# Two tiles in turn for the key differences of shared maxima, the second at the place of a residual block that waits in memory

## The chip, the cores and the metric

The kernel runs on one core of a Trainium2 chip. The metric is the device time of one execution in microseconds (us), the median of three runs. The engines of the core have one instruction queue each: TensorE (PE for its matmuls, PEld for its weight loads), VectorE (DVE), ScalarE (ACT), GpSimd (POOL) and SyncE (SP), which issues all DMAs here. They run side by side and wait for each other through semaphores.

## The reference, cut to what matters

Four layers work on one sequence of S = 2048 rows of D = 576 numbers, all in float32, with H = 32 heads of Dh = 18. Layers 0 and 2 (A) have their own keys and values for each head, layers 1 and 3 (B) share one key and one value head among all 32 query heads.

```
x = x + A(layernorm(x));  x = x + B(layernorm(x))
x = x + A(layernorm(x));  x = x + B(layernorm(x))

A: q, k, v = (x @ wqkv), 32 heads of 18 each
B: q = x @ wq (32 heads), k = x @ wk, v = x @ wv (one head of 18)
scores = (q @ k.T) * 18 ** -0.5
p = softmax(scores, over the keys)
result = (p @ v, heads side by side) @ wo
```

The softmax subtracts each row's maximum, so a maximum over 2048 keys is wanted for each of the 32 x 2048 query rows before the exponentials of that row can be computed.

## The kernel before, in words

**Stages.** The residual x stays in SBUF for the whole kernel, as 16 blocks of 128 rows x 576 (the tile xo, block c is xo[:, c, :]). A layer has a projection stage (layernorm, q and k written to memory, v kept in SBUF), an attention stage, and an output projection that adds its result to xo block by block, block 15 last; this runs together with the next layer's beginning. Between the layernorm statistics of a layer and its output projection, no instruction of the kernel before reads or writes xo.

**Two passes over the scores.** Attention goes over 16 pairs of heads and, in each, over four stretches u of 512 queries: 64 stretches a layer. Each stretch needs 32 score matmuls for its maxima (items m: 128 queries x 512 keys, tile psm in PSUM, max_mm) and 32 for its exponentials (items e: 128 keys x 512 queries, tile pse, exp_mm). The maxima are made LEAD = 14 steps of four items ahead of the exponentials. An e goes through ACT (L826), which writes the exponential into a tile pt, one of a ring of 14; PE multiplies the pt with v into the accumulator oacc (L864). Of an m, DVE takes the maximum of each row (L606).

**Shared maxima.** For some pairs of key blocks the kernel uses max(s0, s1) = s0 + relu(s1 - s0). The matmul of the difference uses differences of keys, prepared on GpSimd (L590, in A layers for the pair of heads after). ACT writes the positive part into the tile relu in SBUF (L599), and a later m, the partner, adds it to its own scores and takes the maximum in one DVE instruction (L604, tensor_tensor_reduce, with a short read of the accumulator behind it). ACT so takes a share of what two DVE reductions would do. Only one tile relu is there: 128 x 512, in the ring "xh". ACT may write it only when the partner before has been consumed on DVE. The partner of a difference is the first item m of the same head that stands more than three items behind it.

**The order** on the engines is written out by hand in the table UNIT, whose round of ten rows makes 32 items m and 32 items e. In an entry such as r12, the letter is the kind (m, e, or r for the m whose matmul is a difference), the first digit is the head of the pair, the second is the rank of the PSUM bank to take, counted from the one used longest ago (`lru`, seven banks). The number behind a row is the count of columns of the product with v that follow the row on PE.

```
        ("e00 e10 m00 r12 m10 e01", 384),
        ("m00 e10 e01 m10 m11 r00", 448),
        ("e00 m10 e00 m01 e10 m01 e10", 416),
        ("e10 m00 m10 m10 e00 e10 e00", 416),
        ("m00 e10 e02 e10 m01 r10 m00", 352),
```

These are rows 5 to 9. A round holds three differences: r12 in row 5, whose partner is the m11 of row 6; r00 in row 6, whose partner is the first m00 of row 8; r10 in row 9. The two heads use different halves of the array's rows, so an item of head 0 and one of head 1 run side by side.

**Differences in the first stretches.** Differences are used from the third stretch of the first pair of heads on, so 62 of 64 stretches in each layer hold three of them: 62 x 3 x 4 = 744 in the kernel.

**Slots of pt.** `slot` chooses which tile of the ring the next exponential goes to. It keeps, in `wrote`, the tick at which each tile was last written by ACT, and in `seen` the last tick that ACT is known to have finished; a difference tile has an entry of its own there.

**The SP queue.** Stores and loads are issued in the program's order. The dictionary `todo` gives steps to them: `run_todo` issues all that is due at the present step, and a transfer that has to wait for another engine holds those behind it. At the start of an attention stage (step LEAD) the queue gets the loads of key differences (diff_in, L637), the constant rows of the next operands (L501, L504) and the next heads' rows (L510); at its end stand the parts of the last stretches (L888 to L910) and the first loads of the output projection (out_rows, L308 and L309).

Of the kernel before, what the change touches and what calls it, by code (L numbers as in the profile page):

```python
# [8 lines left out]
F32 = mybir.dt.float32  # L9
# [7 lines left out]
S, D, H = 2048, 576, 32  # L17
DH = D // H
P = 128
# [27 lines left out]
LEAD = 14  # L47
# [10 lines left out]

OUT_AHEAD = 2
TAIL = 2  # L60

# [18 lines left out]
def tile_kernel(ctx: ExitStack, tc: tile.TileContext, A_x, A_wqkv, A_wo, B_x, B_wq, B_wk, B_wv, B_wo, out):  # L82
    nc = tc.nc
# [6 lines left out]
    dram = ctx.enter_context(tc.tile_pool(name="dram", bufs=1, space=DRAM))  # L90
# [19 lines left out]
    xo = cst.tile([P, NCH, D], F32, name="xo")  # L110
# [25 lines left out]
    m_d = [dram.tile([4, 2, 4, P], F32, name=f"m_d{i}") for i in range(4)]  # L136
    o_d = dram.tile([D, S], F32, name="o_d")
    r_d = dram.tile([H, S], F32, name="r_d")

    rb = cst.tile([P, 512], F32, name="rb")  # L140

# [10 lines left out]
    def bank(i, name):  # L152
        lru.remove(i)
        lru.append(i)
        return psum.tile([P, 512], F32, tag=f"b{i}", bufs=1, name=name)
# [225 lines left out]
    def run_tail(n):  # L381

        for _ in range(n):
            if tail:
                for f, args in tail.pop(0):
                    f(*args)

    def out_proj(last):

        for c in range(NCH):  # L390
# [5 lines left out]
            if c >= OUT_AHEAD:  # L396
                run_tail(TAIL)
            if last and c == NCH - 1:
# [12 lines left out]
    for layer in range(4):  # L411
# [125 lines left out]
        def ops(p):  # L537
            return big[:, q_slot(p)], big[:, k_slot(p)]
# [11 lines left out]
        for a in range(2):  # L550
            n = -4 * LEAD % 32
# [10 lines left out]
        def max_place(a, i):  # L562

            p, u = divmod(i // 16, 4)
            if i < len(m_first):
                return (0, *m_first[i])
            n = i % 16
            return (p, u, *m_order[a][n]) if i >= 32 else (p, u, n // 2 % 4, n // 8 % 2 * 2 + n % 2)


        ns = STEPS * 4 * NPAIR
        m_heads = ([0, 1] * (2 * LEAD) + [a for _, a in UNIT_M] * (4 * NPAIR))[:4 * ns]

        def max_mm(bank=mtile):

            i = m_done[0]
            a = m_heads[i]
            p, u, qc, kb = max_place(a, m_next[a])
            q, k = ops(p)
            if (p, u) not in mxs:  # L580
                mxs[p, u] = pool.tile([P, 32], F32, name="mx") if (p, u) < (0, 2) else mx2[u % 2]
            mx, ps = mxs[p, u], bank("psm")
            by_act = reader[lru[-1]]
            reader[lru[-1]] = False
            b, r = 64 * a, 16 * a + 4 * qc + kb
            c0 = u * 512 + qc * P
            if (p, u) >= (0, 2) and (a, qc, kb) in m_diff:
                assert kd_pair[p % 2 if is_a and p else 2] == (p if is_a else 0)
                k = kd(p)[b:b + 3 * DH]
                nc.tensor.matmul(ps.rearrange("p (h t) -> p h t", h=2) if p == 0 or not is_a else ps,  # L590
                                 q[b:b + 3 * DH, c0:c0 + P], k,
                                 start=True, stop=True)
                t = relus[p, u, a, qc] = relu[:, :512]
                reader[lru[-1]] = True
                if not by_act:
                    seen[0] = max(seen[0], wrote.get("relu", -1))
                wrote["relu"] = ticks[0]
                ticks[0] += 1
                nc.scalar.activation(t, ps, AF.Relu)  # L599
            else:  # L600
                nc.tensor.matmul(ps, q[b:b + KM, c0:c0 + P], k[b:b + KM, kb * 512:(kb + 1) * 512], start=True, stop=True)  # L601
                if kb == 0 and (p, u, a, qc) in relus:
                    t = relus.pop((p, u, a, qc))
                    nc.vector.tensor_tensor_reduce(t, ps, t, 1.0, LOWEST, OP.add, OP.max, mx[:, r:r + 1])  # L604
                else:
                    nc.vector.reduce_max(mx[:, r:r + 1], ps, axis=AX.X)  # L606
            m_next[a] += 1
            m_done[0] += 1
            while m_full and i >= m_full[0][1] + 2:
                max_final(*m_full.pop()[0])  # L610
            m_count[p, u] = m_count.get((p, u), 0) + 1
            if m_count[p, u] == 32:
                assert m_next[0] == m_next[1]
                m_full.append(((p, u), i))

        relus, diffs, kd_pair = {}, {}, {}
        ring, free, wrote, seen, ticks = [], [], {}, [-1], [0]

        def kd(p):
            if p == 0 or not is_a:  # L620
                return big[:, 1::4, 7 * 256:]
            i = p % 2
            return xx_flat[:, 512 * i:512 * i + 512]
# [43 lines left out]
        def max_pairs():  # L667

            if is_a:
                run_todo(m_done[0] // 4)  # L670
            elif m_done[0] == 44:
                max_store(0, 0)
            elif m_done[0] == 48:
                max_rows(0, 0)
            for i in range(4):
                max_mm(etile if i == 3 else mtile)
            while m_full:
                max_final(*m_full.pop()[0])
# [116 lines left out]
        def max_final(p, u):  # L795
            neg = pool.tile([P, 8], F32, name="neg")
            nc.vector.tensor_reduce(neg, mxs.pop((p, u)).rearrange("p (b k) -> p b k", k=4), axis=AX.X, op=OP.max,  # L797
                                    negate=True)
            hl = nms[p, u] = hls[(4 * p + u) % 2]
            copy(nc.gpsimd, hl[:, 0:8], neg)  # L800
            nc.gpsimd.tensor_tensor(hl[:, 8:16], neg, hl.bitcast(F32)[:, 0:8], op=OP.subtract)
# [109 lines left out]


        relu, raw = (pool.tile([P, 640], F32, tag="xh", bufs=2, name=n) for n in ("relu", "raw"))
        todo = {}

        def at(b, f, *args):
            todo.setdefault(b, []).append((f, args))

        for p in range(NPAIR):
            for u in range(4):  # L920
                b = STEPS * (4 * p + u) + STEPS - 1
                if is_a or p or u:
                    at(b + NM_AT, max_store, p, u)
                    at(b + ROW_AT, max_rows, p, u)
                for d, f in ((SUM_AT, o_sum), (L_AT, l_part), (INV_AT, l_inv), (R_AT, l_out), (RB_AT, l_rows),
                             (MUL_AT, o_mul), (O_AT, o_out)):
                    at(b + LEAD + d, f, p, u)
            if p + 1 < NPAIR and is_a:
                for d, f in ((0, diff_in), (3, diff_split), (5, diff_out), (10 if p else 8, diff_rows)):
                    at(max(LEAD, 32 * p - 8) + d, f, p + 1)  # L930
            if is_a and p in (0, 1):
                at(LEAD + 20 + 32 * p, load_rows, q_slot(p + 1), 2 * (p + 1) * DH, DH, 1536, S)
            if p + 1 < NPAIR:
                for i in range(4 if is_a else 2):
                    at(LEAD + 32 * (p - 1) + 1 + 8 * i if p else LEAD + 1 + 4 * i, load_part, p + 1, i)
# [37 lines left out]
        while m_done[0] < 4 * ns:  # L973
            rows, cols = UNIT[phase % len(UNIT)]
            run_todo(LEAD + sum(e_next) / 4)
            for kind, a, rank in rows:
                if kind == "e":
                    exp_next(a, rank)
                elif m_done[0] < 4 * ns:
                    max_mm(oldest(rank))  # L980
            skip = min(cols, PV_LAG - lagged)
            lagged += skip
            pv_cols(cols - skip)
            phase += 1
# [47 lines left out]
```

## Time and profile before

| | us |
|---|---|
| median of three runs | 5727.78 |
| lowest and highest | 5721.95, 5728.45 |
| the profiled execution | 5725.34 |
| span of the profiled execution, first to last instruction | 5723.6 |

| engine | busy, us | share of the span |
|---|---|---|
| PE | 5606.4 | 98% |
| PEld | 3067.1 | 54% |
| DVE | 5026.7 | 88% |
| ACT | 4831.2 | 84% |
| POOL | 1842.7 | 32% |

The granted clock of TensorE was 0.999 on average. The first layer's attention lasts from about 220 to 1430 us, the second's from about 1595 us on.

How to read the rows: a group row names the line, the engine, the operation, its output and input tiles with their sizes and the count; behind it stand the busy time and the mean duration in ns, and, after the bar, how long the engine stood idle just before these instructions and what ended most of that. A row of the timeline gives the start in us from the span's start, the duration in us of all that it merges (the count is at the end, as x3), the engine and the line; in brackets stands the idle time of the engine ahead of it and the instruction whose end released it. A row of waits reads "engine, line <- who was waited for: us in total, times, longest". A window row gives, for each engine, busy time and count of instructions, then the granted clock, the DMA share and GB/s. Matmuls are pipelined and their ends are modelled.

### The profile page before, as it was taken

The numbers are of one execution on the slowest core, as the hardware profiler recorded it, in microseconds if no ns is written. First come the engines' busy times: TensorE is split into PE (matmuls) and PEld (weight loads), VectorE is DVE, ScalarE is ACT, GpSimd is POOL, SyncE is SP. The second block draws the span as 40 slices with busy tenths as digits, with TensorE's granted clock in tenths as the row PEclk, the third lists the DMA queues.
The fourth block names the chain that finished last, engine by engine and source line by source line (L and its number), as shares of the span: only waits on it lengthen the run. The fifth ranks groups of instructions, "written<-read, shape, count | busy, mean of one in ns | idle before, by whom it ended". The sixth has DMA issues, their size and how long they took to land.

```text
span 5723.6 us, 143368 instructions
## 1 busy us (share of the span) xinstructions
PE 5606.4 (98%) x55774; PEld 3067.1 (54%) x55774; DVE 5026.7 (88%) x9489; ACT 4831.2 (84%) x9624; POOL 1842.7 (32%) x2396
## 2 busy tenths in 40 slices
PE   9999999999999999999999999999999999999999
PEld 8644444444844444444686444444448444444446
DVE  4799999998699999999737999999977999999995
ACT  2599999999389999999626999999992999999996
POOL 3243333334233333323412433333342332323232
PEclk9999999999999999999999999999999999999999
DMA  6321111111421000000253211111114100000002
GB/s 204 120 59 41 42 46 44 43 44 27 130 62 26 23 24 20 21 23 24 60 172 102 55 46 41 44 44 46 38 38 132 51 24 23 24 24 20 23 15 79
DMA packets 276207, 303.69 MB, mean 53 GB/s; under 512 B 136270, under 2 KB 194214, under 8 KB 266238
## 3 DMA queue, kind: packets, MB, share of 16 engines
q1 hardware_dynamic: 275526, 294.53, 18.0%
q8 instruction: 438, 7.18, 0.5%
q14 instruction: 243, 1.99, 0.1%
HBM read 168.50 MB, written 121.95 MB: 51 GB/s over the span
## 4 chain that ended last, share of the span: by engine, by line
PE 85%; DVE 8%; ACT 3%; issue 2%; POOL 1%; DMA 0%; SPq 0%; ACTq 0%; POOLq 0%; DVEq 0%
PE oacc L864 33%; PE psm L601 21%; PE pse L822 19%; PE psn L259 6%; DVE mx L606 5%; PE psq L433 5%; ACT relu L599 3%; DVE relu L604 3%; PE psm L590 1%; ACT pt L826 0%; POOL ev L445 0%; PE ps L251 0%; DMA big<-qk_d 0%; POOL wsm L205 0%; PE oacc L252 0%
## 5 line engine op out<-in xcount | busy, mean ns | idle before, releaser
L826 ACT ACTIVATE pt<-pse 128x512 f32<-128x512 f32 x8192 | 4233.6, 620 | 104.8 <-PE pse L822 86.0
L606 DVE TENSOR_REDUCE mx<-psm 128x1 f32<-128x512 f32 x6704 | 4183.3, 684 | 81.6 <-PE pse L822 49.0
L601 PE MATMUL psm<-big 62*128 62x512 f32 x7448 | 2461.4, 430 | 91.5 <-ACT relu L599 88.8
L822 PE MATMUL pse<-big 64*128 64x512 f32 x8192 | 2537.5, 442 | 1.7 <-ACT evr L444 1.6
L864 PE MATMUL oacc<-pt,vbuf 128*19 128x416 f32 (+9 forms) x26544 | 1733.0, 368 | 4.6 <-DVE oc L176 4.0
L822 PEld LDWEIGHTS pse<-big 64*128 64x128 f32 x8192 | 1214.0, 184 | 796.8 <-DVE mx L606 370.6
L601 PEld LDWEIGHTS psm<-big 62*128 62x128 f32 x7448 | 1178.7, 185 | 687.2 <-ACT pt L826 251.9
L864 PEld LDWEIGHTS oacc<-pt,vbuf 128*19 128x19 f32 x26544 | 546.4, 97 | 792.4 <-issue 551.9
L176 POOL TENSOR_SCALAR hl<-neg 128x8 fp32r<-128x8 f32 x256 | 50.6, 197 | 2693.1 <-DVE neg L797 2693.1
L604 DVE CUSTOM_DVE_ANT_0 relu<-psm,relu 128x512 f32<-128x512 f32 x744 | 509.4, 685 | 175.7 <-ACT pt L826 173.6
L599 ACT ACTIVATE relu<-psm 128x512 f32<-128x512 f32 x744 | 452.1, 608 | 140.8 <-DVE mx L604 135.2
L864 PE MATMUL oacc<-pt,vy 128*19 128x384 f32 (+3 forms) x8176 | 570.1, 383 | 0.0
L892 POOL TENSOR_TENSOR rl<-lt,mone 128x8 f32<-128x8 f32 x256 | 422.3, 1650 | 297.6 <-DMA lt<-os 291.6
L176 POOL TENSOR_SCALAR os<-oc 32x512 f32<-32x512 f32 x512 | 313.2, 612 | 114.2 <-DVE oc L176 63.6
L441 ACT ACTIVATE ev<-psq 128x512 fp32r<-128x512 f32 (+1 forms) x112 | 66.9, 598 | 326.9 <-PE psq L433 222.8
L883 POOL TENSOR_TENSOR os<-os,oc 96x512 f32<-96x512 f32 x256 | 328.0, 1281 | 21.4
L905 POOL TENSOR_TENSOR os<-os,rb 96x512 f32<-96x512 f32 x256 | 328.7, 1284 | 18.9 <-DMA rb<-r_d 18.9
L259 PE MATMUL psn<-wsm,xx 128*128 128x288 f32 x2240 | 307.9, 296 | 1.3 <-issue 1.3
L259 PEld LDWEIGHTS psn<-wsm,xx 128*128 128x128 f32 x2240 | 298.7, 188 | 14.3 <-issue 12.3
L864 PEld LDWEIGHTS oacc<-pt,vy 128*19 128x19 f32 x8176 | 177.9, 98 | 229.4 <-issue 196.6
L447 DVE TENSOR_TENSOR ev<-psq,ev 128x512 fp32r<-128x512 f32 (+1 forms) x84 | 58.0, 691 | 213.9 <-ACT ev L441 202.6
L433 PE MATMUL psq<-yx,big 128*128 128x512 f32 (+2 forms) x826 | 197.1, 391 | 4.2 <-ACT yx L243 2.2
(93 smaller groups left out, 2391.5 us busy)
## 6 DMA issues: line engine op xcount, KB each, us to landing
big<-qk_d SPq DMA_DIRECT2D x172, 432.0 KB
qk_d<-ev SPq DMA_DIRECT2D x96, 512.0 KB
qk_d<-ev SPq DMA_DIRECT2D x120, 256.0 KB
rb<-r_d SPq DMA_DIRECT2D x512, 36.0 KB
o_d<-os SPq DMA_DIRECT2D x512, 36.0 KB
o<-o_d SPq DMA_DIRECT2D x64, 256.0 KB
xx<-qk_d SPq DMA_DIRECT2D x120, 72.0 KB
big<-m_d SPq DMA_DIRECT2D x512, 4.0 KB
```

The source lines that it names most:

```text
L176: eng.tensor_scalar(dst, src, 1.0, 0.0, op0=OP.mult, op1=OP.add)
L259: nc.tensor.matmul(ps, lhs[:, xc, :], wsm[:, wc, h * 288:(h + 1) * 288], start=i == 0, stop=i == len(TERMS) - 1)
L433: nc.tensor.matmul(ps[:n].rearrange("p (u t) -> p u t", u=2)[:, us], w[:, wc, :n], xts[T][:, us, xc, :], start=(xc, wc) == TERMS[0], stop= ...
L599: nc.scalar.activation(t, ps, AF.Relu)
L601: nc.tensor.matmul(ps, q[b:b + KM, c0:c0 + P], k[b:b + KM, kb * 512:(kb + 1) * 512], start=True, stop=True)
L604: nc.vector.tensor_tensor_reduce(t, ps, t, 1.0, LOWEST, OP.add, OP.max, mx[:, r:r + 1])
L606: nc.vector.reduce_max(mx[:, r:r + 1], ps, axis=AX.X)
L822: nc.tensor.matmul(e, k[r:r + KE, kc * P:(kc + 1) * P], q[r:r + KE, u * 512:(u + 1) * 512], start=True, stop=True)
L826: nc.scalar.activation(pt, e, AF.Exp, scale=SCALE)
L864: nc.tensor.matmul(oacc[j:j + DH + 1, cs], v_of(kc)[:, 2 * p + a if is_a else 0, :], pts[p, u, i][:, cs], start=kc < 2 and c0 == 0, stop=k ...
L892: nc.gpsimd.tensor_tensor(rl, lts.pop((p, u)), mone, op=OP.pow)
L905: nc.gpsimd.tensor_tensor(t[:96], t[:96], rb[:96], op=OP.mult)
```

## The change: what it does

The one tile relu becomes a list of two that are used in turn. The second is the first 512 columns of xo[:, 15, :], the last residual block. So that the block is free during attention, it is stored to a new tensor x_d in memory at step LEAD of each layer, ahead of what else is due at that step, and fetched at step LEAD + ns - 8 (ns = 512), when the last difference has been used. The first difference of each layer takes the place in xo. The tick bookkeeping for the ring of pt now has an entry for each of the two tiles. The matmuls, activations and reductions, and their order, are as before.

```
+AWAY = (15,)
...
+    x_d = dram.tile([len(AWAY), P, D], F32, name="x_d")
...
-                t = relus[p, u, a, qc] = relu[:, :512]
+                j = turn_r[0] = (turn_r[0] + 1) % len(relu)
+                assert all(n != j for n, _ in relus.values())
+                t = relu[j][:, :512]
+                relus[p, u, a, qc] = j, t
                 reader[lru[-1]] = True
                 if not by_act:
-                    seen[0] = max(seen[0], wrote.get("relu", -1))
-                wrote["relu"] = ticks[0]
+                    seen[0] = max(seen[0], wrote.get(-1 - j, -1))
+                wrote[-1 - j] = ticks[0]
                 ticks[0] += 1
                 nc.scalar.activation(t, ps, AF.Relu)
...
-                    t = relus.pop((p, u, a, qc))
+                    _, t = relus.pop((p, u, a, qc))
                     nc.vector.tensor_tensor_reduce(t, ps, t, 1.0, LOWEST, OP.add, OP.max, mx[:, r:r + 1])
...
-        relus, diffs, kd_pair = {}, {}, {}
+        relus, diffs, kd_pair, turn_r = {}, {}, {}, [0]
...
         relu, raw = (pool.tile([P, 640], F32, tag="xh", bufs=2, name=n) for n in ("relu", "raw"))
+        relu = [relu] + [xo[:, c, :] for c in AWAY]
...
+        def x_away():
+            for i, c in enumerate(AWAY):
+                nc.sync.dma_start(x_d[i], xo[:, c, :])
+
+        def x_back():
+            for i, c in enumerate(AWAY):
+                nc.sync.dma_start(xo[:, c, :], x_d[i])
+
+        at(LEAD, x_away)
+        at(LEAD + ns - 8, x_back)
```

## The prediction

> **What bounds the kernel now.** I read the page first: the busy times, the chain of waits, and the groups of the two operations that the edit touches.
>
> ```profile
> span 5723.6 us, 143368 instructions
> PE 5606.4 (98%) x55774; PEld 3067.1 (54%) x55774; DVE 5026.7 (88%) x9489; ACT 4831.2 (84%) x9624; POOL 1842.7 (32%) x2396
> PE 85%; DVE 8%; ACT 3%; issue 2%; POOL 1%; DMA 0%; SPq 0%; ACTq 0%; POOLq 0%; DVEq 0%
> PE oacc L864 33%; PE psm L601 21%; PE pse L822 19%; PE psn L259 6%; DVE mx L606 5%; PE psq L433 5%; ACT relu L599 3%; DVE relu L604 3%; PE psm L590 1%; ACT pt L826 0%; POOL ev L445 0%; PE ps L251 0%; DMA big<-qk_d 0%; POOL wsm L205 0%; PE o
> ...
> L604 DVE CUSTOM_DVE_ANT_0 relu<-psm,relu 128x512 f32<-128x512 f32 x744 | 509.4, 685 | 175.7 <-ACT pt L826 173.6
> L599 ACT ACTIVATE relu<-psm 128x512 f32<-128x512 f32 x744 | 452.1, 608 | 140.8 <-DVE mx L604 135.2
> ```
>
> TensorE (PE) is busy 98%, VectorE (DVE) 88%, ScalarE (ACT) 84%. The chain lies on PE for 85%, but a share leaves it: L606 and L604 on DVE, then L599 on ACT (5%, 3%, 3%). L599 is the ACT activation that writes the positive part of a difference block; L604 is the DVE instruction that reads it. Each runs 744 times, three in each of 248 rounds of the UNIT table.
>
> The window table over 1000 us of attention in an A layer and in a B layer shows an even state.
>
> ```profile
> 300.00:1300.00 1000.00, 981.08 (x10466) 486.71 (x10465) 950.26 (x1778) 948.03 (x1881) 360.02 (x457) 1.00 0.17 45
> 4600.00:5600.00 1000.00, 981.07 (x10469) 486.59 (x10466) 950.73 (x1781) 948.36 (x1882) 305.12 (x370) 1.00 0.09 21
> ```
>
> PE 981, DVE 950 and ACT 948 us of 1000, with the clock granted at 1.00. No engine is full, and none has more than 52 us per 1000 to spare. So I asked the table of waits who waits for whom.
>
> ```profile
> DVE relu L604 <- ACT pt L826: 173.6, 246, 0.7
> ACT relu L599 <- DVE mx L604: 135.2, 241, 0.6
> PE psm L601 <- ACT relu L599: 88.8, 244, 0.7
> ```
>
> ACT stands still ahead of L599 for 135.2 us in 241 waits, 0.56 us each, until L604 is done; PE then stands still for 88.8 us until L599 is done. About one such pair falls in each round. Two neighbouring rounds show where. First ACT, from the timeline:
>
> ```profile
> 2001.36 0.60 ACT L599 ACTIVATE relu<-psm 128x512 f32<-128x512 f32 x1
> 2001.84 1.60 ACT L826 ACTIVATE pt<-pse 128x512 f32<-128x512 f32 x3
> 2004.00 0.60 ACT L599 ACTIVATE relu<-psm 128x512 f32<-128x512 f32 x1 [0.56 <-DVE mx L604]
> 2004.49 5.58 ACT L826 ACTIVATE pt<-pse 128x512 f32<-128x512 f32 x11
> 2009.95 0.62 ACT L599 ACTIVATE relu<-psm 128x512 f32<-128x512 f32 x1
> ...
> 2023.12 0.60 ACT L599 ACTIVATE relu<-psm 128x512 f32<-128x512 f32 x1 [0.56 <-DVE mx L604]
> ```
>
> The round lasts 2023.12 - 2004.00 = 19.12 us. Of its three L599, those at 2001.36 and 2009.95 (r12 and r10 of the table) show no wait; the one at 2004.00 (r00) waits 0.56. DVE in the same stretch:
>
> ```profile
> 2003.22 0.68 DVE L604 CUSTOM_DVE_ANT_0 relu<-psm,relu 128x512 f32<-128x512 f32 x1
> ...
> 2003.90 1.98 DVE L606 TENSOR_REDUCE mx<-psm 128x1 f32<-128x512 f32 x3
> 2006.59 0.69 DVE L604 CUSTOM_DVE_ANT_0 relu<-psm,relu 128x512 f32<-128x512 f32 x1 [0.71 <-ACT pt L826]
> ...
> 2012.36 6.13 DVE L606 TENSOR_REDUCE mx<-psm 128x1 f32<-128x512 f32 x10 [0.19 <-PE pse L822]
> ```
>
> The L604 at 2003.22 consumes r12's tile and ends, with its 0.08 us read of the accumulator, at 2003.90; r00 begins 0.10 us later. The weights of r00's own matmul were loaded at 2002.02 (first row of the next fence), so only the tile held it. Later DVE waits 0.71 us, until 2006.59. Then the weight loads of PE (PEld), which show when PE reaches each burst of score matmuls:
>
> ```profile
> 2002.02 0.18 PEld L590 LDWEIGHTS psm<-big 54*128 54x128 f32 x1
> ...
> 2003.33 0.18 PEld L822 LDWEIGHTS pse<-big 64*128 64x128 f32 x1
> ...
> 2003.67 0.18 PEld L601 LDWEIGHTS psm<-big 62*128 62x128 f32 x1
> 2004.65 0.18 PEld L601 LDWEIGHTS psm<-big 62*128 62x128 f32 x1 [0.80 <-ACT relu L599]
> ...
> 2005.08 0.14 PEld L864 LDWEIGHTS oacc<-pt,vbuf 128*19 128x19 f32 x8 [0.25 <-issue]
> 2005.91 0.18 PEld L822 LDWEIGHTS pse<-big 64*128 64x128 f32 x1 [0.69 <-ACT pt L826]
> ...
> 2006.48 0.31 PEld L822 LDWEIGHTS pse<-big 64*128 64x128 f32 x2
> 2007.04 0.20 PEld L864 LDWEIGHTS oacc<-pt,vbuf 128*19 128x19 f32 x16 [0.25 <-issue]
> ```
>
> Table row 7 holds seven score matmuls and takes 2005.08 - 2003.33 = 1.75 us; row 8 holds seven as well, four for one half of the array and three for the other like row 7, and takes 2007.04 - 2005.91 = 1.13. The extra 0.62 us sits ahead of the load at 2004.65, which waits for L599: it takes over the PSUM bank of r00. The chain in each round is thus L604, L599, row 7, and everything behind it.
>
> **The change part by part.** *Second tile.* L599 takes two tiles in turn, so r00 no longer waits for the L604 at 2003.22 but for the one that read the other tile, about half a round earlier. Nothing is added to or taken from the instructions of PE, ACT and DVE. What comes free per round is read on each engine:
>
> - ACT: r00 could start when the three activations from 2001.84 have issued. That is at least 0.56 us earlier; up to 0.12 more, since activations overlap when nothing holds them (2001.36 to 2001.84 is 0.48 for a duration of 0.60).
> - PE: row 7 can shrink by 0.62, to the 1.13 of row 8. r00 would start between 2003.32 and 2003.44 and end by 2004.04; PE wants its bank at 2004.65 - 0.62 = 2004.03, so L599 is late there by 0.06 at most, with the hop to PE.
> - DVE: the work behind 2006.59 can come 0.71 earlier; then its gap is gone.
> - What is late next: in the bank order that the table gives, the sixth matmul of row 8 takes the bank of the sixth of row 7, the last of the three L606 from 2003.90, which end at 2005.88. That matmul's load is one of the pair at 2006.48. Moved by 0.62 it would come at 2005.86, before that bank is free; with the 0.05 us that L599's end at 2004.60 takes to reach the load at 2004.65, it can come at 2005.93. So the round shortens by 0.55.
>
> The value I take is 0.55 us in each of 248 rounds: 136 us. Bounds: 0.62 x 248 = 154 us if that bank costs nothing, and PE's own idle time, 88.8 us, if the burst has less slack than its loads show. Behind row 8 each engine keeps its present distance to the others, since all follow PE's shift; so I look for no new wait there.
>
> For the same wait the matmul's own row books 0.36 us of idle PE, where the loads show 0.62:
>
> ```profile
> 2004.65 0.50 PE L601 MATMUL psm<-big 62*128 62x512 f32 x1 [0.36 <-ACT relu L599]
> ```
>
> The Trainium skill ("Perfetto Trace Analysis", Identifying the Most-Contended Engine) says that the busy share of matmuls is a poor measure of how near TensorE is to its limit, because they are pipelined. By that rule the 88.8 us is no ceiling; against it, with PE's busy row taken at its word, the sum would be 88.8. The trace agrees with the rule so far as the two figures of this one wait differ.
>
> *Where the second tile lies, and its trips.* Residual block 15 is stored once a layer (x_away) and fetched once (x_back), 128 x 576 x 4 bytes = 288 KB each, on SP's queue. No engine instruction touches the block meanwhile. x_away goes in at the start of attention, ahead of the loads of L637:
>
> ```profile
> 219.71 0.33 SPq L469 DMA_DIRECT2D qk_d<-ev  x1
> 220.12 3.45 SPq L637 DMA_DIRECT2D xx<-qk_d  x4
> 225.76 0.61 ACT L599 ACTIVATE relu<-psm 128x512 f32<-128x512 f32 x1
> 1424.03 0.41 SPq L308 DMA_DIRECT2D o<-o_d  x1
> 1426.59 0.43 DVE L176 TENSOR_SCALAR xx<-o 128x512 fp32r<-128x512 f32 x1 [2.68 <-DMA o<-o_d]
> ```
>
> The first L599 of the layer, at 225.76, gets the new tile and so waits for x_away's landing. L309's and L308's 256 KB loads show the time of such a transfer: issued at 1424.03, used at 1426.59, 2.6 us. From 220.1 that gives 223 us, 2.7 us before it is wanted. I take nothing; the bound is twice the transfer, which still gives 225.3, and one more such transfer ahead of it, 3 us in each of four layers: 12 us. Behind x_away stand on SP the loads of L637 and the others of the next head pair, which shift by one issue, 0.3 to 0.8 us; the difference rows of pair 1 are wanted some 30 steps on, so nothing of it is seen. x_back comes at the end, when the difference tiles are no longer used; ahead of the o loads it can cost one issue and one transfer, some 0.4 + 2.6 us a layer, 12 us again. SP has room there: in the first layer it stands from 1416.58 to 1420.94.
>
> ```profile
> 1416.06 0.52 SPq L811 DMA_DIRECT2D big<-m_d  x2
> 1420.94 0.61 SPq L895 DMA_DIRECT2D r_d<-rl  x1
> ```
>
> So I take nothing. The block is wanted only by the last chunk of the output projection.
>
> *Slots.* The choice of the ring slot for exp tiles reads the tick of the tile's last L599, which is now older, so more activations may carry a wait of their own.
>
> ```profile
> L826 ACTq EVENT_SEMAPHORE  x876: 17/17/1129, 217.3 to 5657.5; - x176
> ```
>
> Such a wait takes 17 ns; one more a round is 4 us. I take nothing, with 4 us as the other bound, and as much to the good side if a slot choice comes out better.
>
> Sum, on the profiled execution's own time: it took 5725.3 us (span 5723.6 and 1.7 around it), and 5725.3 - 136 = 5589. It lay 2.5 us under the median of the three runs, 5727.8, so the forecast is 5591, or 2.4% less.
>
> **The rivals.** *Only PE's recorded idle time comes back.* If the matmuls behind the wait run at their limit in a way that the loads hide, 88.8 us is all: 5728 - 89 = 5639. For it: PE is busy 981 of 1000, and 0.36 x 248 = 89. Against it: rows 7 and 8 issue the same number of matmuls, and the 1.13 is seen in row 8 in the same round.
>
> *Row 8's bank costs nothing and overlap on ACT is won back too:* 0.62 a round, 5574.
>
> *The wait stays, or another takes its place in full.* The tile would be tracked together with the whole residual array, or r00 would be held by DVE's order through its bank: 5728. For it: DVE is busy 950 of 1000 and r00's release always coincides with L604. Against it: DVE has 0.71 + 0.19 us of gaps in the round, more than the 0.56, and the only users of the array during attention are L599, L604 and the two transfers.
>
> *Slower, by the clock.* The TensorE clock is granted by a regulator, and one stretch shows it low:
>
> ```profile
> 3072.00:3074.00 2.00, 2.00 (x14) 0.83 (x6) 0.77 (x2) 0.40 (x2) 0.00 (x0) 0.50 0.32 96
> ```
>
> At 0.50 for two us, with PE shown as busy throughout, ACT and DVE nearly stop. If a denser PE made such stretches common in attention, a round of 19.12 - 0.55 = 18.57 us at full clock would stretch; it is back at 19.12 at a mean clock of 18.57 / 19.12 = 0.971, and slower from there on: at 0.95 it is 19.55, 0.43 x 248 = 106 us over, 5834. Against it: in both windows above PE is already at 98% with 1.00 granted.
>
> **How the numbers follow.** Chances: the forecast with its own range of 5574 to 5610, 0.60; overlap won back, 5574 or a little below, 0.10; only the recorded idle time, near 5639, 0.15; wait stays, 0.07; slower, 0.04; the remaining 0.04 for losses at the layers' ends that leave between 5645 and 5716. Against no change I take a bound of 0.2%, 11 us, about what a measurement of this kernel can tell. Faster holds the first three and the last: 0.89. Same takes 0.06 of the case in which the wait stays, and slower its last 0.01 with the clock's 0.04: 0.05. The range runs from 5566 (154 and the 4 us of slots to the good, and the spread of the runs) to 5645 (the recorded idle time with some us of the layers' ends).
>
> **What would show it.** In the table of waits, ACT relu L599 <- DVE mx L604 should fall from 135.2 us to near nothing, PE psm <- ACT relu from 88.8 likewise. The round should be near 18.57 us, row 7 near 1.13 to 1.2 us, DVE's 0.71 us gap near 0.1, and row 8 should show up to 0.1 more. DVE and ACT should come to some 978 and 976 of 1000 (950 and 948 x 19.12 / 18.57). The first L599 of a layer should show no wait for a transfer. I am wrong if the round stays near 19.1 with another name in ACT's wait, if row 7 shrinks and another row grows by as much, or if the granted clock falls below 1.00 in attention.

## The result and the profile after

The changed kernel takes 5558.8 us (median of four runs, 5556.9 to 5563.9), the kernel before 5725.6 in the same comparison: a ratio of 0.971, with a 95% interval of 0.9694 to 0.9727. The profiled execution has a span of 5555.7 us, 167.8 less than before. The forecast was 5591 and the range began at 5566; the gain is larger than both allow. Of the kernels below, one (early_two) had one run of 19033.8 us among its six, far from the other five (5557.6 to 5560.6), and it is read by these five. First the page of the changed kernel, with the busy times and the chain of waits:

```profile
span 5555.7 us, 143125 instructions
PE 5524.8 (99%) x55774; PEld 3101.2 (56%) x55774; DVE 5001.2 (90%) x9489; ACT 4814.6 (87%) x9624; POOL 1844.3 (33%) x2396
PE 95%; issue 1%; POOL 1%; ACT 1%; DMA 1%; DVE 0%; SPq 0%; POOLq 0%; ACTq 0%; DVEq 0%
PE oacc L871 38%; PE pse L829 23%; PE psm L608 21%; PE psn L263 6%; PE psq L437 5%; PE psm L594 2%; ACT pt L833 0%; POOL ev L449 0%; PE ps L255 0%; DVE mx L613 0%; POOL wsm L209 0%; POOL big L209 0%; DMA big<-qk_d 0%; DMA qk_d<-ev 0%; POOL 
```

The chain has come back to PE: 95%, where it was 85%, and the DVE and ACT lines that made up the detour (5%, 3%, 3%) are gone. The change moved the lines: L599 is now L606, L604 is L611, L606 is L613, L601 is L608, L822 is L829, L826 is L833, L864 is L871. The window table over 1000 us of an A layer and of a B layer:

```profile
300.00:1300.00 1000.00, 997.68 (x10824) 510.72 (x10823) 978.18 (x1841) 978.38 (x1949) 374.99 (x479) 1.00 0.17 46
4450.00:5450.00 1000.00, 999.85 (x10860) 512.98 (x10858) 980.92 (x1847) 980.85 (x1955) 315.37 (x383) 1.00 0.09 22
```

DVE and ACT were forecast at 978 and 976 of 1000 and stand at 978 to 981; PE, at 981 before, is at 998 to 1000, all with the clock at 1.00. What ACT waited for ahead of the activation that writes a difference tile is told by the view of that line:

```profile
L606 ACT ACTIVATE xo<-psm x372: 605/620/664, 224.6 to 5450.8; 128x512 f32<-128x512 f32 x186
L606 ACT ACTIVATE relu<-psm x372: 605/620/662, 226.5 to 5456.9; 128x512 f32<-128x512 f32 x186
its engine sat idle before it (us, times) until:
who waited for it (us, times):
busy tenths in 40 slices 0010101010001010111000010101000001011010
```

Below "its engine sat idle" and "who waited for it" no row stands any more: the 135.2 us of ACT and the 88.8 us of PE are gone to the last. Now the round, on ACT, in the changed kernel:

```profile
2000.65 0.61 ACT L606 ACTIVATE xo<-psm 128x512 f32<-128x512 f32 x1
2001.13 1.60 ACT L833 ACTIVATE pt<-pse 128x512 f32<-128x512 f32 x3
2002.56 0.66 ACT L606 ACTIVATE relu<-psm 128x512 f32<-128x512 f32 x1
...
2019.07 0.60 ACT L606 ACTIVATE relu<-psm 128x512 f32<-128x512 f32 x1
```

r00 (2002.56) starts while the last of the three exponentials ahead of it is still running (they end at 2001.13 + 1.60 = 2002.73), and the round lasts 2019.07 - 2000.65 = 18.42 us, against 19.12 before. On DVE the gap ahead of r00's partner went from 0.71 to 0.18 us:

```profile
2005.26 0.69 DVE L611 CUSTOM_DVE_ANT_0 relu<-psm,relu 128x512 f32<-128x512 f32 x1 [0.18 <-PE psm L608]
```

The weight loads of PE show the rows 6, 7, 8 and 10 of the table (a row reaches from its first score load to the first load of L871 behind it):

```profile
2000.83 0.18 PEld L608 LDWEIGHTS psm<-big 62*128 62x128 f32 x1 [0.21 <-DVE mx L613]
...
2001.74 0.14 PEld L871 LDWEIGHTS oacc<-pt,vbuf 128*19 128x19 f32 x8 [0.24 <-issue]
...
2002.62 0.18 PEld L829 LDWEIGHTS pse<-big 64*128 64x128 f32 x1
...
2003.75 0.14 PEld L871 LDWEIGHTS oacc<-pt,vbuf 128*19 128x19 f32 x8 [0.24 <-issue]
2004.58 0.18 PEld L829 LDWEIGHTS pse<-big 64*128 64x128 f32 x1 [0.69 <-ACT pt L833]
...
2005.76 0.19 PEld L871 LDWEIGHTS oacc<-pt,vbuf 128*19 128x19 f32 x16 [0.24 <-issue]
...
2008.44 0.18 PEld L608 LDWEIGHTS psm<-big 62*128 62x128 f32 x1 [0.37 <-ACT pt L833]
...
2009.70 0.62 PEld L871 LDWEIGHTS oacc<-pt,vbuf 128*19 128x19 f32 x16 [0.24 <-issue]
```

Row 7 falls from 1.75 to 1.13 us and row 8 grows from 1.13 to 1.18, both as forecast in size. But row 6 (2000.83 to 2001.74) now takes 0.91 us and row 10 (2008.44 to 2009.70) 1.26. In the kernel before they took 0.97 and 1.31:

```profile
2001.47 0.18 PEld L601 LDWEIGHTS psm<-big 62*128 62x128 f32 x1 [0.21 <-DVE mx L606]
2002.44 0.14 PEld L864 LDWEIGHTS oacc<-pt,vbuf 128*19 128x19 f32 x8 [0.24 <-issue]
2009.73 0.18 PEld L601 LDWEIGHTS psm<-big 62*128 62x128 f32 x1 [0.37 <-ACT pt L826]
2011.04 0.62 PEld L864 LDWEIGHTS oacc<-pt,vbuf 128*19 128x19 f32 x16 [0.24 <-issue]
```

These 0.06 us each, in two rows of every round, were not in the forecast. The round is 0.70 us shorter and not 0.55: 0.62 from row 7, less 0.05 in row 8, and 0.06 each from rows 6 and 10. By the medians that is 0.696 x 248 = 173 us, of which the span shows 168.

### The profile page after: what moved, and what is told of

Read it like the earlier page. It is cut to its first block, busy times and chain, and to the rows that moved or that the text cites. A ratio compares the mean times of both kernels' runs of the same rounds, so it can differ in the third digit from the quotient of the medians.

```text
span 5555.7 us, 143125 instructions
## 1 busy us (share of the span) xinstructions
PE 5524.8 (99%) x55774; PEld 3101.2 (56%) x55774; DVE 5001.2 (90%) x9489; ACT 4814.6 (87%) x9624; POOL 1844.3 (33%) x2396
## 4 chain that ended last, share of the span: by engine, by line
PE 95%; issue 1%; POOL 1%; ACT 1%; DMA 1%; DVE 0%; SPq 0%; POOLq 0%; ACTq 0%; DVEq 0%
PE oacc L871 38%; PE pse L829 23%; PE psm L608 21%; PE psn L263 6%; PE psq L437 5%; PE psm L594 2%; ACT pt L833 0%; POOL ev L449 0%; PE ps L255 0%; DVE mx L613 0%; POOL wsm L209 0%; POOL big L209 0%; DMA big<-qk_d 0%; DMA qk_d<-ev 0%; POOL wsm L180 0%
## 5 line engine op out<-in xcount | busy, mean ns | idle before, releaser
L833 ACT ACTIVATE pt<-pse 128x512 f32<-128x512 f32 x8192 | 4218.8, 624 | 96.1 <-PE pse L829 80.5
L613 DVE TENSOR_REDUCE mx<-psm 128x1 f32<-128x512 f32 x6704 | 4173.7, 684 | 65.9 <-PE psm L608 14.9
L829 PE MATMUL pse<-big 64*128 64x512 f32 x8192 | 2528.5, 443 | 2.6 <-ACT evr L448 1.6
L608 PE MATMUL psm<-big 62*128 62x512 f32 x7448 | 2397.4, 427 | 4.3 <-DVE mx L613 2.0
L871 PE MATMUL oacc<-pt,vbuf 128*19 128x416 f32 (+9 forms) x26544 | 1733.6, 368 | 4.6 <-DVE oc L180 4.0
L829 PEld LDWEIGHTS pse<-big 64*128 64x128 f32 x8192 | 1227.8, 184 | 798.8 <-DVE mx L613 369.6
L608 PEld LDWEIGHTS psm<-big 62*128 62x128 f32 x7448 | 1180.2, 185 | 508.8 <-ACT pt L833 251.9
L871 PEld LDWEIGHTS oacc<-pt,vbuf 128*19 128x19 f32 x26544 | 546.8, 97 | 785.5 <-issue 545.8
L871 PE MATMUL oacc<-pt,vy 128*19 128x384 f32 (+3 forms) x8176 | 570.1, 383 | 0.0
L871 PEld LDWEIGHTS oacc<-pt,vy 128*19 128x19 f32 x8176 | 177.9, 98 | 223.3 <-issue 190.5
L611 DVE CUSTOM_DVE_ANT_0 relu<-psm,relu 128x512 f32<-128x512 f32 x372 | 254.7, 685 | 23.5 <-PE psm L608 16.9
L611 DVE CUSTOM_DVE_ANT_0 xo<-psm,xo 128x512 f32<-128x512 f32 x372 | 254.7, 685 | 21.7 <-PE psm L608 19.9
L606 ACT ACTIVATE relu<-psm 128x512 f32<-128x512 f32 x372 | 234.0, 629 | 0.0
```

The costliest lines, as they stand in the source:

```text
L829: nc.tensor.matmul(e, k[r:r + KE, kc * P:(kc + 1) * P], q[r:r + KE, u * 512:(u + 1) * 512], start=True, stop=True)
L833: nc.scalar.activation(pt, e, AF.Exp, scale=SCALE)
L871: nc.tensor.matmul(oacc[j:j + DH + 1, cs], v_of(kc)[:, 2 * p + a if is_a else 0, :], pts[p, u, i][:, cs], start=kc < 2 and c0 == 0, stop=k ...
```

## The experiments

All kernels were timed beside the kernel before. The table gives the total and, from each kernel's trace, the median of the round (from one r12 on ACT to the next, within a layer) and of rows of the UNIT table over the 248 rounds.

| kernel | total, us | round | row 6 | row 7 | row 8 | row 10 | row 1 |
|---|---|---|---|---|---|---|---|
| before | 5725.6 | 19.12 | 0.97 | 1.75 | 1.14 | 1.32 | 0.90 |
| changed | 5558.8 | 18.42 | 0.91 | 1.13 | 1.18 | 1.26 | 0.90 |
| r00_second | 5557.9 | 18.42 | 0.91 | 1.13 | 1.19 | 1.26 | 0.90 |
| r10_second | 5711.7 | 19.05 | 0.90 | 1.82 | 1.14 | 1.26 | 0.90 |
| three_tiles | 5560.9 | 18.42 | 0.91 | 1.13 | 1.19 | 1.27 | 0.90 |
| early_partner | 5590.6 | 18.53 | 0.96 | 1.16 | 1.15 | 1.32 | 0.90 |
| old_ticks | 5590.1 | 18.53 | 0.96 | 1.13 | 1.19 | 1.32 | 0.90 |
| new_ticks | 5710.0 | 19.05 | 0.90 | 1.82 | 1.14 | 1.26 | 0.90 |
| early_new | 5569.6 | 18.46 | 0.91 | 1.22 | 1.14 | 1.26 | 0.90 |
| early_two | 5558.9 | 18.42 | 0.91 | 1.13 | 1.18 | 1.26 | 0.90 |
| r10_half | 5555.2 | 18.39 | 0.90 | 1.13 | 1.19 | 1.13 | 1.00 |
| cols_9_10 | 5580.3 | 18.50 | 0.91 | 1.13 | 1.19 | 1.15 | 1.09 |

**Whose wait it was.** Two kernels give the second tile to one difference of the round only. They differ from the changed kernel in one line:

```
-                j = turn_r[0] = (turn_r[0] + 1) % len(relu)
+                turn_r[0] = (turn_r[0] + 1) % 3
+                j = int(turn_r[0] == 2)        (r00_second; r10_second: == 0)
```

> Changed kernel, but only r00 uses the second tile; r12 and r10 share the first. Theory (the whole gain is r00's wait for the tile): as the changed kernel, 5559 us (5550 to 5570), round 18.42 us. Rival (the turn itself matters: r12 and r10 gain too, or the ring slots of pt chosen with it): less of the gain, between 5600 and 5726 us.

> Changed kernel, but only r10 uses the second tile; r12 and r00 share the first, so r00 waits for r12's partner as before. Both memory trips and the new bookkeeping stay. Theory: no gain, 5726 us (5715 to 5740), ACT's wait ahead of the activation 135 us again; what it lies over the kernel before is the price of the trips. Rival (gain from bookkeeping or from the tile's place): near 5559 us.

With the second tile for r00 alone the whole gain is there: 5557.9 us. With it for r10 alone r00 waits on r12's tile as before. So the gain by tiles is r00's. But r10_second did not come to 5726: it is 14 us faster than the kernel before, 0.9975 with an interval of 0.9965 to 0.9984, though the wait of ACT ahead of the difference's activation (L607 here) is there in full. The view of that line:

```profile
its engine sat idle before it (us, times) until:
  PE pse L830: 147.9, 235
...
who waited for it (us, times):
  PE psm L609: 106.0, 248
```

Its r00 waits even longer (row 7 is 1.82 us; PE's idle time behind it 106 us instead of 88.8), and yet rows 6 and 10 are the short ones of the changed kernel. The view names an e matmul as the releaser, but the rows of DVE and ACT put the accumulator read of r12's partner, which ends at 2004.04, just ahead of r00:

```profile
2003.35 0.68 DVE L612 CUSTOM_DVE_ANT_0 relu<-psm,relu 128x512 f32<-128x512 f32 x1
2003.96 0.08 DVE L612 DVE_READ_ACCUMULATOR2_ANT mx<- 128x1 f32 x1
```

```profile
2004.13 0.60 ACT L607 ACTIVATE relu<-psm 128x512 f32<-128x512 f32 x1 [0.63 <-PE pse L830]
```

So rows 6 and 10 can't have shortened because r00 stopped waiting. Something else in the edit does it.

**More tiles, more trips.** Blocks 14 and 15 both go away, and three tiles are used in turn.

```
-AWAY = (15,)
+AWAY = (14, 15)
```

> Changed kernel with blocks 14 and 15 both away, three tiles in turn. Theory (with two tiles no difference waits any more, and the trips are hidden): as the changed kernel, 5559 us (5552 to 5568), with the doubled trips costing 0 to 5 us. Rival (tiles still wait somewhere): 10 us or more below; rival (the trips cost something, the part of the round's gain that the total lacks): 5 to 15 us above.

5560.9 us, within the spread of the changed kernel: a third tile brings nothing, and a second pair of trips a layer costs at most some 2 us in all. The first pair costs no more: r10_second with trips and new_ticks (below) without them have the same rows and the same round, and are 1.7 us apart. The trips were rightly taken at nothing.

**The same release without a second tile.** The kernel before, with r12's partner one DVE instruction earlier.

```
-  ... if at_ > own[i][0] + 3 and not x and not order[j])] = qc, 0
+  ... if at_ > own[i][0] + 3 - a and not x and not order[j])] = qc, 0
```

> Kernel before with its one tile and no memory trip; for head 1 the partner stands at least three instead of more than three items behind its difference, so r12's partner is the fourth item of row 6 instead of the fifth, one DVE instruction (0.6 us) earlier; r10's and r00's stay. Theory (only the end of r12's partner against ACT's readiness matters): ACT's wait falls from 0.56 us to 0.1 or less, 5555 to 5585 us without a second tile. Rival (a second tile is needed, or the earlier partner makes DVE wait for ACT's r12): 5650 us or more.

5590.6 us, just above what the theory gave. ACT's wait for the tile is gone with one tile:

```profile
its engine sat idle before it (us, times) until:
  DVE mx L604: 2.0, 3
```

2.0 us in place of 135.2. So what cost these 135 us was the order of two instructions, not the number of tiles. But rows 6 and 10 stay at 0.96 and 1.32 here.

**What shortens rows 6 and 10.** Two theories were put against each other. O: ACT runs ahead by 0.06 us, because its activations overlap again when r00 is not held. S: the ring's bookkeeping chooses other slots for the exponentials, and these need fewer waits. r10_second already speaks against O. The next three runs separate the parts: the changed kernel with the bookkeeping of before (old_ticks), the kernel before with the bookkeeping alone (new_ticks), and the earlier partner with the bookkeeping (early_new; both without a second tile or trips).

```
old_ticks, against the changed kernel:
-                    seen[0] = max(seen[0], wrote.get(-1 - j, -1))
-                wrote[-1 - j] = ticks[0]
+                    seen[0] = max(seen[0], wrote.get("relu", -1))
+                wrote["relu"] = ticks[0]
new_ticks and early_new, against the kernel before (early_new has also the "+ 3 - a"; turn_r starts at [0]):
+                j = turn_r[0] = (turn_r[0] + 1) % 2
                 t = relus[p, u, a, qc] = relu[:, :512]
-                    seen[0] = max(seen[0], wrote.get("relu", -1))
-                wrote["relu"] = ticks[0]
+                    seen[0] = max(seen[0], wrote.get(-1 - j, -1))
+                wrote[-1 - j] = ticks[0]
```

> Changed kernel with two tiles and trips, but the ring of pt is told of both tiles through the one entry of the kernel before (wrote["relu"]), so the slots are chosen as before. Theory S (the change gained twice: 0.58 us a round from r00's wait, 0.12 from slots that no longer put an extra wait on two exponentials for which ACT stands idle): rows 6 and 10 of the table go back to 0.97 and 1.32 us, round 18.54, total 5588 us (5580 to 5596). Rival O (rows 6 and 10 shrank because ACT overlaps its activations again once r00 is not held): slots make no difference, 5559 us.

> Kernel before with one tile and no trip, only the ring's bookkeeping of the changed kernel (two entries in turn). Theory S: rows 6 and 10 shorten by 0.06 each, r00's wait on the tile takes half of it back, round 19.05, 5711 us (5704 to 5718). Rival O: nothing changes, 5726 us.

> One tile, no trip: the earlier partner of r12 together with the two-entry bookkeeping. Theory S: both gains without a second tile, round 18.42 us, as the changed kernel: 5559 us (5550 to 5566), a few us less if the trips cost anything. Rival O: as the earlier partner alone, 5590 us.

S holds in the first two: old_ticks takes 5590.1 us, with rows 6 and 10 back at 0.96 and 1.32, and new_ticks 5710.0. The tiles alone thus bring 5725.6 - 5590.1 = 135 us, and the bookkeeping on top of them 31 us; on the kernel before, where r00's wait eats half of it again (row 7 from 1.75 to 1.82), 16 us. The views of the exponentials' line show what the bookkeeping does, first in the changed kernel, then in old_ticks:

```profile
L833 ACTq EVENT_SEMAPHORE  x632: 17/17/1129, 216.1 to 5489.7; - x158
```

```profile
L833 ACTq EVENT_SEMAPHORE  x876: 17/17/1129, 217.0 to 5523.3; - x176
```

An exponential may overwrite a slot of pt when ACT's own last write of it is known to be done. Where it is not known, the program waits for that write as well, and the second wait stands in an instruction of its own, of 17 ns, ahead of the activation. There are 632 of these in the changed kernel and 876 in old_ticks, as in the kernel before: 244 fewer, one a round (two of a round go and one comes in elsewhere). Why the other choice of slots leaves fewer of them was not followed. All kernels of the table divide by this count: those with 876 (before, early_partner, old_ticks) have row 6 at 0.96 or 0.97 and row 10 at 1.32, the others have 632, and row 6 at 0.90 or 0.91 and row 10 at 1.27 or less. The price of a separate wait shows where ACT has nothing to do until PE's matmul is done, as ahead of the two exponentials before r12. ACT in the changed kernel, then in old_ticks, then in the kernel before:

```profile
2018.10 1.09 ACT L833 ACTIVATE pt<-pse 128x512 f32<-128x512 f32 x2 [0.18 <-PE pse L829]
```

```profile
2015.59 1.09 ACT L833 ACTIVATE pt<-pse 128x512 f32<-128x512 f32 x2 [0.23 <-PE pse L829]
```

```profile
2000.39 1.09 ACT L826 ACTIVATE pt<-pse 128x512 f32<-128x512 f32 x2 [0.23 <-PE pse L822]
```

The exponential that starts at 2018.10 carries PE's wait itself, and ACT stands idle 0.18 us ahead of it. In the two others the matmul's wait is a separate instruction, the activation starts only behind it, and ACT stands idle 0.23. The plainer measure is the time from the start of an exponential's matmul to the start of its activation, as the median over the rounds: ahead of r12 it is 0.53 us in all kernels of the table with 632 waits and 0.59 in the three with 876. At the first of the three exponentials ahead of r10, the other place where a separate wait goes, it is 0.56 or 0.57 against 0.62 or 0.63. The wait instruction itself takes 17 ns of these 60; what the rest is, no row shows. In a stretch where ACT is backlogged the separate wait is passed before ACT is free, and costs nothing: the one that comes in elsewhere stands in such a stretch, and the spacing of the activations there stays at 0.48. Behind a separate wait that ends last, ACT comes 0.06 us later to r12, and so does PE to the bank that r12 holds; in the changed kernel and in the kernel before, r00's load, the last of row 6, starts 0.05 us behind r12's end. The same holds for r10 and the last load of row 10.

early_new came to 5569.6 us, 4 us above its range. It has the short rows 6 and 10, but row 7 at 1.22. Its r00 is seldom booked as waiting for the tile:

```profile
  DVE mx L605: 3.8, 8
```

Only 3.8 us are booked as idle time, but the loads of row 7 show 0.09 us a round. That fits an ACT that comes 0.06 us sooner to r00 and so uses up the margin that the earlier partner gave; there the second tile is worth 11 us.

**What is left in row 10.** In the changed kernel row 10 takes 0.12 us more than row 9 (1.13). Two kernels try to take this away. In one, r10's activation covers 256 of its 512 columns, so a part of the maxima is left out; in the other 64 columns of the product with v move from behind row 10 to behind row 9.

```
r10_half (turn_r starts at [0, 0]):
-                nc.scalar.activation(t, ps, AF.Relu)
+                turn_r[1] = (turn_r[1] + 1) % 3
+                w = 256 if turn_r[1] == 0 else 512
+                nc.scalar.activation(t[:, :w], ps[:, :w], AF.Relu)
cols_9_10:
-        ("m00 e10 e02 e10 m01 r10 m00", 352),
-        ("m11 e00 e10 m01 m10 e11 e00", 384)]
+        ("m00 e10 e02 e10 m01 r10 m00", 416),
+        ("m11 e00 e10 m01 m10 e11 e00", 320)]
```

> Changed kernel in which r10's activation covers only 256 of its 512 columns, so the maxima of that block are partly wrong; all else is kept. If row 10's last matmul waits for ACT to be done with r10's bank, it comes up to 0.2 us earlier: row 10 falls from 1.26 to about 1.13 us, round 18.30, 5529 us (5520 to 5545). If the 0.12 us is PE's own order of the two heads, row 10 stays at 1.26 and the total within 5 us of 5559.

> Changed kernel with 64 columns of the product with v moved from behind row 10 to behind row 9 (352 to 416, 384 to 320), all work kept. If the 0.12 us that row 10 is still longer than row 9 is a wait for ACT to read r10's bank, row 10 reaches it later and shrinks from 1.26 to 1.13 us: round 18.30, 5529 us (5522 to 5545). If it is PE's own order, or ACT is the bound (98% busy), no gain: 5559 us.

Both theories were half right. Row 10 falls to 1.13 and 1.15 us, so its excess is the wait for ACT to read r10's bank. But row 1, next in the round, grows from 0.90 to 1.00 and to 1.09, as the loads of row 1 in r10_half show:

```profile
2013.26 0.18 PEld L610 LDWEIGHTS psm<-big 62*128 62x128 f32 x1 [0.16 <-DVE mx L615]
...
2013.83 0.18 PEld L831 LDWEIGHTS pse<-big 64*128 64x128 f32 x1
2014.26 0.14 PEld L873 LDWEIGHTS oacc<-pt,vbuf 128*19 128x19 f32 x8 [0.25 <-issue]
```

The totals, 5555.2 and 5580.3 us, are not the 5529 that I gave. With DVE and ACT at 98%, the next wait stands just behind, and the traces show that it is DVE's. By the bank order of the table, the last matmul of row 1 takes the bank of row 10's m10. In r10_half DVE reads that one as a partner:

```profile
2013.09 0.68 DVE L613 CUSTOM_DVE_ANT_0 xo<-psm,xo 128x512 f32<-128x512 f32 x1
2013.69 0.08 DVE L613 DVE_READ_ACCUMULATOR2_ANT mx<- 128x1 f32 x1
```

It ends at 2013.77, and the last load of row 1 starts at 2013.83. Over the rounds this load comes 0.06 us behind that end in the changed kernel, in r10_half and in cols_9_10 alike, and 0.45, 0.58 and 0.66 us behind the first load of row 1: what PE gains in row 10 it waits for there. Two more kernels took the columns for row 9 from behind row 2 instead (480 to 448 and 416).

> Changed kernel with 32 columns of the product with v (0.07 us) moved from behind row 2 to behind row 9. Where the wait of row 10 for ACT is covered and row 3 has slack on DVE and ACT, row 10 falls to 1.19 us and the round by 0.06: 5543 us (5538 to 5552). If DVE (98% busy) holds rows 3 to 6 then, no gain or up to 10 us more: 5559 to 5570.

> The same with 64 columns (0.13 us): 5530 us (5525 to 5545) if rows 3 to 6 have the slack, and 5565 to 5590 if what row 10 gains is lost again there, as it was in row 1 when the columns came from behind row 10.

They took 5959.9 and 5934.6 us, far outside every case. Row 10 does fall in them, to 1.20 and 1.15 us, and row 1 grows to 0.93 and 0.98, as in the two kernels above; but the totals say nothing on this: the columns of rows 1 and 2 are what the product with v trails by, so a stretch no longer ended at the end of a row, and PE stood behind ACT's copy of the accumulator. The waits of the first:

```profile
PE oacc L871 <- ACT oc L880: 364.1, 244, 1.5
```

That is 1.5 us in each of 244 stretches, 364 of the 401 us that this kernel takes more than the changed one.

**Both together.** The changed kernel with the earlier partner (the "+ 3 - a" above):

> Changed kernel (two tiles, trips, new bookkeeping) with r12's partner one DVE instruction earlier, as in the run with the earlier partner. Row 8 was 1.18 us with the partner as the fifth item and 1.14 with the fourth. Theory (row 8 waits for the last reduction of row 7 on DVE, and the earlier partner moves nothing on PE): row 8 falls by 0.05, round 18.37, 5547 us (5543 to 5553). Rival (the 0.05 comes back in another row, since DVE and ACT are 98% busy): 5559 us.

5558.9 us, as the changed kernel, and row 8 stays at 1.18. The theory was badly made, twice. DVE works through the same instructions in the same time, so an earlier partner does not let the last reduction of row 7 end earlier. And it is not DVE that holds row 8. In the changed kernel the last reduction of row 7, the last exponential of row 7 and the last two loads of row 8 are (one row each of the engines' timelines):

```profile
2004.39 0.68 DVE L613 TENSOR_REDUCE mx<-psm 128x1 f32<-128x512 f32 x1
2004.66 0.62 ACT L833 ACTIVATE pt<-pse 128x512 f32<-128x512 f32 x1
2005.16 0.18 PEld L829 LDWEIGHTS pse<-big 64*128 64x128 f32 x1
2005.34 0.18 PEld L829 LDWEIGHTS pse<-big 64*128 64x128 f32 x1
```

By the bank order the sixth matmul of row 8 (2005.16) takes the bank that DVE's reduction frees, the seventh (2005.34) the bank of the exponential, which ends at 2005.28. Over the rounds the sixth load stands at 0.58 us into the row before the change and after it. The seventh comes 0.05 us behind the end of the exponential before the change and after it, and goes from 0.70 to 0.76 us into the row. So the growth of row 8 is a wait for ACT. No version tried beats the changed kernel by more than the spread of its runs.

## Why the prediction was wrong, and where it was right

**Wrong: the term "Slots".** It said of the ring's bookkeeping that "more activations may carry a wait of their own", priced one at 17 ns, took nothing, and set 4 us as the bound to both sides. It was 31 us to the good on top of the tiles (old_ticks, 5590.1, against 5558.8), and that alone carried the time below the range: with the old bookkeeping the time lies 1 us from the forecast. Two mistakes lie in it. The sign was guessed: I did not follow which exponentials carry a separate wait in the kernel before, and there came to be 244 fewer of them, not more. And the price was taken from the wait's own duration of 17 ns, where each of the two that went away on ACT's way to r12 and r10 was worth 0.06 us of the round. Nor were rows 6 and 10 looked at: I took their length as PE's own, though two rows that I had quoted told of r00 waiting for r12's bank: r12 ended at 2001.36 + 0.60 = 2001.96, and the load of r00 came at 2002.02.

**Right: the tiles.** The step "second tile" gave 0.55 us a round and 136 us. Alone (old_ticks) it brings 0.58 us a round and 135 us. Row 7 did shrink by 0.62, ACT's and PE's waits are gone, and DVE's gap closed to 0.18 where I said near 0.1. That the total meets the forecast to 1 us is in part luck: 0.58 x 248 = 144 us by rounds is more than the 135 of the total, since two rounds in the A layers are longer in the fast kernels (in old_ticks by 5.3 and 1.9 us; last section).

**Right in size, by luck: row 8.** I put 0.07 us there for the bank of the last reduction on DVE, and the row grew by 0.05. But that bank was free in time: its load kept its place in the row. What grew the row is the bank of row 7's last exponential on ACT, which held the last load of row 8 in the kernel before already and which I had not looked at. The seven hundredths and the five have different causes.

**Wrong in a sentence: the neighbours.** "Behind row 8 each engine keeps its present distance to the others" held for the tiles (in old_ticks rows 6 and 10 stay at 0.96 and 1.32) but not for the edit as a whole, since ACT comes nearer to PE with the other slots.

**The rivals.** That only PE's recorded idle time of 88.8 us comes back is out: it was 135 from the tiles alone, so the weight loads gave the better measure of that wait than the idle time of the matmuls. After the change PE shows 998 to 1000 us busy of 1000, and row 10 still holds 0.12 us of waiting for ACT. The Trainium skill's rule that the busy share of matmuls is a poor measure of how near TensorE is to its limit ("Perfetto Trace Analysis", Identifying the Most-Contended Engine) agrees with both. The clock stayed at 1.00 in attention. The wait did not stay, and the trips cost nothing beyond the spread of the runs.

## What to carry to other kernels

Where one buffer is handed between two engines that are both nearly full, look which end is late: moving the consumer one instruction ahead brought 135 of 167 us without the second buffer. A separate wait instruction cost nothing here while its engine was backlogged and about 0.06 us where what it waits for came last, so in a loop of hundreds of rounds it matters where the extra waits fall; a rule that chooses slots by which writes are known to be done belongs among the priced terms of a change. And in a balanced loop a released wait can come back in a later row, as in rows 8 and 1 here: measure the round, not the row.

## What had not been expected of the hardware

The separate waits are the one thing: 17 ns of their own, and 0.06 us from the start of the matmul to the start of the activation where that matmul is what ACT waits for. The other is in the first and third layers: one round early in attention takes longer in the changed kernel (21.9 us at 336 us and 21.6 at 3102, against 18.42), and likewise in the other kernels whose rounds came to 18.53 us or less (20.0 to 23.8), but not in the kernel before, r10_second or new_ticks, where the longest stand at 0.8 us or less over the median. In the waits between 330 and 362 us of the changed kernel stand:

```profile
POOL wsm L180 <- DMA raw<-in_A_wo_dram: 12.5, 2, 7.3
...
DVE tr L813 <- POOL hl L808: 2.3, 1, 2.3
```

GpSimd stands for up to 7.3 us for the weights of the output projection, and what DVE wants from it is 2.3 us late. Before, the longest such wait in the same window was 5.6 us and DVE's row is not there. That a round that is shorter leaves the loads less time is a possible reason, but it was not tried.
